# An attention and channel-mix kernel: queries kept four tokens a row, two batches turned on TensorE in FP32, finer tasks in a new order

## The chip, the cores and the metric

One core of a Trainium2 chip runs the whole program. The time is device time in microseconds (us). Executions of one kernel mostly differ by 1 to 2% (four of the kernel before took 282.42 to 286.85 us), so each run below is given as the median of its executions, beside executions of the kernel before on the same chip in the same rounds. A ratio is the mean time of one kernel's runs over that of the other's runs of the same rounds, so it is not quite the ratio of the medians quoted. Engines: PE is TensorE's matmuls, PEld its weight loads, DVE is VectorE, ACT ScalarE, POOL GpSimd. The "granted clock" is the share of TensorE's full clock that its throttle allowed.

## What the kernel computes

Eight batches of eight heads, 576 tokens, head size 64. Attention is causal in blocks of 64 tokens; its output, 512 wide, goes through a channel mix.

```python
scores = np.matmul(q, k.transpose(0, 1, 3, 2)) / np.sqrt(D)
scores = np.where(block_i >= block_j, scores, -1e9)      # blocks of 64 tokens
attn = np.exp(scores - np.max(scores, axis=-1, keepdims=True))
x = np.matmul(attn / np.sum(attn, axis=-1, keepdims=True), v)
# ... heads side by side: x is [8, 576, 512]; x_prev is x one token earlier
xk = mu_k * x + (1 - mu_k) * x_prev
xr = mu_r * x + (1 - mu_r) * x_prev
k = np.maximum(xk @ w_k, 0.0)                            # 512 -> 1024
out = sigmoid(xr @ w_r) * ((k * k) @ w_v)                # 1024 -> 512
```

## The kernel before

Every engine is given its instructions in an order that a planner writes at build time. The planner keeps a list of tasks (a few matmuls, one exponential, one load), lets them go in a simulation with guessed durations, and writes them out in that order. Five parts matter here.

**Turning.** The score matmuls take queries and keys with the head dimension on the partitions (64 partitions x 512 in the trace). Batches 2 to 7 are cast to bf16 and turned by DMA. Batches 0 and 1 (`LONGS = 2`) are cast, turned on TensorE in bf16 and copied out of PSUM:

```python
for j in range(JT):                       # add_long_qkt, batches 0 and 1
    nc.tensor.matmul(pst[:, j * D:(j + 1) * D],
                     tiles["nb", b, g, n][y * D:(y + 1) * D, j],
                     identb[...], is_transpose=True, ...)
```

**Denominators and values.** For each batch and each half (four heads), `sums()` adds up the exponentials and `part(i)` multiplies them with the values. Both use weights 32 columns wide, dealt to four column groups of TensorE, so that four small matmuls run side by side (in the trace of the kernel before, those of a group of four mostly start 3 to 5 ns apart):

```python
for t in range(3):                        # sums(): three thirds of the tokens
    ...
    for g in range(G):
        nc.tensor.matmul(PS[g * R:g * R + R, q0 - a:W3],
                         THIRD[:, (3 - t) % 3:(3 - t) % 3 + R],
                         probs(b, 4 * Q + g, kc, q0, z - q0), ...,
                         tile_position=(0, g * R))
```

This makes 119 matmuls for each batch and half. They stand in two tasks, the second free to go later.

**Normalizing** is one VectorE multiplication of a PSUM tile by the spread reciprocals, written where the channel mix reads it.

**Channel mix.** Chunks of 512 tokens: tasks of four (`w_k`, `w_r`) or eight (`w_v`) matmuls of 512 columns, 0.22 us each (0.216 us from start to start at full clock).

**Fillers.** 300 matmuls with the identity are put where TensorE would idle at the start, to keep its clock up.

## Time and profile before

| | kernel before |
|---|---|
| time | 283.6 us, median of 3 (282.59 to 286.85) |
| span of the profiled run | 282.1 us |
| TensorE busy | 93% |
| TensorE instructions in the trace (weight loads, matmuls and 12 of its sequencer) | 6,932 |
| first channel-mix matmul | 48.40 us |

The prediction below shows the lines of this profile on which it rests. The list of what TensorE waited for (what was waited for, total us, times, longest us) begins so:

```profile
PE t_s L538 <- ACT t_e L560: 3.6, 5, 1.0
PE t_m L469 <- POOL t_nl L286: 3.1, 1, 3.1
```

Each entry names what was late: another engine or a DMA. For matmuls, which this list counts, no entry of this kernel says "issue" (its weight loads, which start 0.08 us before their matmuls in the median, do have such entries, 20.7 us of them at L538). "Issue" is how the profile marks idle time for which it finds nothing that was waited for. The second part is one line of the list of DMA queues (transfers, MB, share):

```profile
q8 instruction: 27, 0.44, 0.7%
```

By its name this queue brings the program itself. It moved 27 transfers of 0.44 / 27 MB, about 16 KB each, and 6,932 TensorE instructions are 27 times 256.

### The profile page before, as it was taken

How to read it: one execution, taken by the hardware profiler on the slowest of the kernel's cores; microseconds unless marked ns; L12 is line 12 of the kernel's file. 1: busy time of each engine (PE TensorE's matmuls, PEld its weight loads, DVE VectorE, ACT ScalarE, POOL GpSimd, SP SyncE). 2: the span in 40 equal slices, each digit the busy share in tenths (PEclk: the TensorE clock that was granted, in tenths of full speed). 3: DMA queues.
4: the chain of work that ended last, by engine and by line, in shares of the span. 5: the costliest groups of instructions: out<-in, count | busy, mean ns of one | idle time of the engine just before them, and what ended most of it. 6: DMA issues, size and time to landing. Idle time of an engine off the chain costs nothing. (4 is left out here: it accounts for less than half of the span.)

```text
span 282.1 us, 8552 instructions
## 1 busy us (share of the span) xinstructions
PE 261.7 (93%) x3460; PEld 137.7 (49%) x3460; DVE 215.1 (76%) x395; ACT 186.3 (66%) x268; POOL 125.1 (44%) x262
## 2 busy tenths in 40 slices
PE   8999856898999987999999999989999999997995
PEld 8977543343445442545444545435545445543443
DVE  1663689599946986889999948893999599996432
ACT  1379778469299756875998689558865980450530
POOL 4125685076054404383475426755833532640220
PEclk9999997599999997999999999999999999999999
DMA  6999999794999899998999899999979103102113
GB/s 187 372 240 250 288 325 216 161 214 73 214 238 221 202 210 240 187 196 208 230 194 198 189 267 202 195 235 232 187 144 274 46 1 111 44 0 76 74 39 112
DMA packets 137112, 51.43 MB, mean 182 GB/s; under 512 B 127728, under 2 KB 127984, under 8 KB 137072
## 3 DMA queue, kind: packets, MB, share of 16 engines
q1 hardware_dynamic: 137072, 50.88, 77.6%
q8 instruction: 27, 0.44, 0.7%
q14 instruction: 13, 0.11, 0.1%
HBM read 33.56 MB, written 9.44 MB: 152 GB/s over the span
## 5 line engine op out<-in xcount | busy, mean ns | idle before, releaser
L560 ACT ACTIVATE t_e<-t_s 128x1024 f16<-128x1024 f32 x96 | 96.0, 1024 | 23.2 <-PE t_s L538 23.0
L786 PE MATMUL t_mm<-t_xk,WK 128*128 128x512 f16 x288 | 68.7, 383 | 1.4 <-POOL t_xk L765 0.9
L848 PE MATMUL t_mm<-WV,t_k 128*128 128x512 f16 (+1 forms) x296 | 66.8, 374 | 1.1 <-DVE t_o L858 1.0
L568 POOL MEMSET t_e<- 64x128 f16 x128 | 24.9, 210 | 73.1 <-ACT t_e L560 70.3
L796 ACT ACTIVATE t_kr<-t_mm 128x512 f32<-128x512 f32 x72 | 42.4, 599 | 17.5 <-PE t_mm L786 14.8
L848 PEld LDWEIGHTS <-t_k 128*128 128x128 f16 x296 | 27.9, 98 | 34.6 <-issue 3.8
L786 PEld LDWEIGHTS <-WK 128*128 128x128 f16 x288 | 26.2, 98 | 34.7 <-issue 7.4
L805 DVE TENSOR_TENSOR t_k<-t_kr 128x512 f16<-128x512 f32 x37 | 29.0, 796 | 18.4 <-ACT t_kr L796 18.2
L829 ACT ACTIVATE t_t<-t_mm 128x512 f32<-128x512 f32 x36 | 21.6, 600 | 31.8 <-PE t_mm L819 31.6
L819 PE MATMUL t_mm<-WR,t_xr 128*128 128x512 f16 x144 | 38.9, 401 | 1.9 <-DVE t_o L858 1.2
L538 PE MATMUL t_s<-t_qkt 64*128 64x64 bf16 (+4 forms) x384 | 34.0, 283 | 5.3 <-ACT t_e L560 3.6
L805 POOL TENSOR_TENSOR t_k<-t_kr 128x512 f16<-128x512 f32 x24 | 28.3, 1187 | 23.3 <-ACT t_kr L796 22.8
L750 DVE SCALAR_TENSOR_TENSOR t_xk<-t_d,MUK,t_xt 128x512 f16<-128x512 f32 x36 | 33.5, 945 | 3.0 <-POOL t_d L738 2.6
L858 DVE SCALAR_TENSOR_TENSOR t_o<-t_t,t_mm 128x512 f32<-128x512 f32 (+1 forms) x37 | 24.7, 666 | 12.0 <-PE t_mm L848 7.1
L750 DVE SCALAR_TENSOR_TENSOR t_xr<-t_d,MUR,t_xt 128x512 f16<-128x512 f32 x36 | 30.9, 874 | 0.0
L738 POOL TENSOR_TENSOR t_d<-t_xt 128x512 f32<-128x512 f32 x16 | 21.0, 1313 | 13.7 <-DVE t_xt L688 13.3
L538 PEld LDWEIGHTS <-t_qkt 64*128 64x128 bf16 x384 | 12.9, 95 | 27.8 <-issue 20.7
L688 DVE TENSOR_TENSOR t_xt<-t_m,t_rd 128x384 f32<-128x384 f32 (+3 forms) x42 | 22.2, 549 | 5.3 <-PE t_m L608 5.2
L608 PEld LDWEIGHTS <-VO 128*32 128x32 f16 x1264 | 23.3, 98 | 5.8 <-issue 5.3
L608 PE MATMUL t_m<-t_e,VO 128*32 128x192 f16 (+3 forms) x976 | 24.6, 243 | 0.0
L888 PE MATMUL t_mm<-identb 128*128 128x128 bf16 x300 | 21.9, 230 | 2.2 <-POOL identb masks.py:199 1.4
L819 PEld LDWEIGHTS <-t_xr 128*128 128x128 f16 x144 | 13.3, 101 | 20.7 <-issue 6.6
(58 smaller groups left out, 251.4 us busy)
## 6 DMA issues: line engine op xcount, KB each, us to landing
out_dram<-t_o SPq DMA_DIRECT2D x35, 256.0 KB, 2.9
t_vl<-in_v_dram SPq DMA_DIRECT2D x32, 256.0 KB, 4.9
t_ld<-in_q_dram SPq DMA_DIRECT2D x48, 128.0 KB, 3.6
t_ld<-in_k_dram SPq DMA_DIRECT2D x48, 128.0 KB, 3.6
t_ld<-in_q_dram SPq DMA_DIRECT2D x8, 288.0 KB, 6.7
t_ld<-in_k_dram SPq DMA_DIRECT2D x8, 288.0 KB, 6.0
t_ld<-in_moe_w_k_dram SPq DMA_DIRECT2D x8, 256.0 KB, 5.3
t_ld<-in_moe_w_v_dram SPq DMA_DIRECT2D x8, 256.0 KB, 5.0
```

The lines of the kernel that those rows point to most:

```text
L538: nc.tensor.matmul(PS[:, h, col:col + n], qkt[rows, pr, 1, kc * P:kc * P + P], qkt[rows, pr, 0, q0:q0 + n], start=True, stop=True)
L560: nc.scalar.activation(tiles["e", b, pr][:, :, i, :], tiles["ps", b, it], AF.Exp, scale=ISQ)
L568: nc.gpsimd.memset(tiles["e", b, pr][D:P, :, i, z:z + D], 0.0)
L608: nc.tensor.matmul(ps[g * R:g * R + R, q0 - a:z - a], lhs(kc, g), probs(b, 4 * Q + g, kc, q0, z - q0), start=(kc == 0 and last is not None ...
L688: nc.vector.tensor_tensor(xt_tile(c)[:, 2 * Q:2 * Q + 2, 1 + at:1 + at + w], tiles["num", b, Q, i][:, 0:2 * w].rearrange("p (s t) -> p s t ...
L750: nc.vector.scalar_tensor_tensor(tiles[name, c][:, cc], tiles["d", c, cc], (MUK1, MUR1)[n][:, cc:cc + 1], tiles["xt", c][:, cc, 1:CH + 1], ...
L786: nc.tensor.matmul(ps, WK[:, cc, jc * P:(jc + 1) * P], tiles["xk", c][:, cc], start=(cc == 0), stop=(cc == CCn - 1))
L796: nc.scalar.activation(tiles["kr", c, jc], tiles["pk", c, jc], AF.Relu)
L805: (nc.vector if eng == "DVE" else nc.gpsimd).tensor_tensor(K2, KR, KR, ALU.mult)
L819: nc.tensor.matmul(ps, tiles["xr", c][:, cc, jt * P:(jt + 1) * P], WR[:, cc], start=(cc == 0), stop=(cc == CCn - 1))
L848: nc.tensor.matmul(ps[:, 0:w], tiles["k2", c][:, jc, jt * P:(jt + 1) * P], WV[:, jc, cols], start=(jc == 0), stop=(jc == JCn - 1))
L858: nc.vector.scalar_tensor_tensor(tiles["o", c, jt, part][:, 0:w], tiles["t", c, jt][:, cols], 1.0, tiles["pv", c, jt, part][:, 0:w], ALU.a ...
```

## The change

The intent: queries are loaded with four neighbouring tokens a row (1 KB pieces) and keep that order up to the normalization, which puts the tokens back in place. Batches 0 and 1 are turned on TensorE straight from the f32 tiles, without casts. Tasks become finer, and TensorE's order is a fixed list in place of ranks. The core of the diff, with cuts marked:

```diff
-LONGS = 2
+TURNED = 2
+TENSOR = """
+q000 q001 q010 q100 q011 s000 q0t q031 s001 s0t0 q030 q021 s010 s030 q020 q1t
...                                   # 339 tasks in TensorE's order
@@ loads of queries (and of keys in batches 0 and 1)
+            return [(d[:, :].rearrange("p (h c) -> p h c", h=2),
+                     src[b, 2 * pr:2 * pr + 2, 0:CUT].rearrange(
+                         "h (p j) d -> p h (j d)", j=J))]
@@ turning batches 0 and 1
+                            nc.tensor.matmul(
+                                PS[h * D:h * D + D, j * P:j * P + P],
+                                tiles["ld", b, pr, n][:, c:c + D], identf,
+                                start=True, stop=True)
@@ denominators: four token groups in place of three thirds
-            for t in range(3):
-                            THIRD[:, (3 - t) % 3:(3 - t) % 3 + R],
+            for j in range(J):
+                for kc in range(J):
+                            FOURTH[:, (J - j) % J:(J - j) % J + R],
@@ values: three tasks of their own, and one for the denominators
-        for v, mine in enumerate(([0], [1, 2])):
+        for den, mine in (True, []), (False, [0]), (False, [1]), (False, [2]):
@@ normalizing puts the tokens back in order
+                            x[:, :, 0:w].rearrange("q s (p j) -> q s j p", j=J),
+                            num[:, :, 0:w].rearrange("q s (j p) -> q s j p", j=J),
```

Each batch and half now has 190 small matmuls on average instead of 119.

## The prediction

> **What bounds the kernel now.** I read the page first: which engine is fullest, and when.
>
> ```profile
> span 282.1 us, 8552 instructions
> PE 261.7 (93%) x3460; PEld 137.7 (49%) x3460; DVE 215.1 (76%) x395; ACT 186.3 (66%) x268; POOL 125.1 (44%) x262
> ...
> PEclk9999997599999997999999999999999999999999
> DMA  6999999794999899998999899999979103102113
> ```
>
> TensorE is the fullest engine, no other passes 76%, and the chain that ended last is TensorE almost alone. But busy is not useful work: 300 of the 3460 matmuls multiply the bf16 identity, fillers that keep the clock up. So I went to the ten-microsecond windows: after "window:" come its length, then PE, PEld, DVE, ACT and POOL busy, granted clock, DMA share, GB/s.
>
> ```profile
> 10.00:20.00 10.00, 9.60 (x189) 8.28 (x187) 5.74 (x9) 5.97 (x10) 2.20 (x4) 1.00 0.97 276
> 30.00:40.00 10.00, 5.71 (x170) 3.87 (x166) 7.86 (x19) 7.67 (x9) 8.17 (x14) 1.00 1.08 309
> 40.00:50.00 10.00, 6.23 (x166) 4.01 (x166) 9.96 (x21) 7.59 (x12) 6.21 (x13) 0.80 0.97 246
> 50.00:60.00 10.00, 9.83 (x104) 4.42 (x105) 6.34 (x14) 5.47 (x9) 2.73 (x5) 0.69 0.90 174
> 150.00:160.00 10.00, 10.00 (x162) 4.90 (x161) 9.92 (x20) 7.79 (x12) 4.41 (x12) 1.00 0.95 189
> ```
>
> From 60 us on TensorE is full: summing its windows, idle from 60 to 279 us is some 7 us. The loss is before: idle from 30 to 50 us is 8 us, and the clock falls to 0.80 and 0.69, which costs 2.0 + 3.1 = 5.1 us (1.7 us more around 105 to 115 us: 0.87 and 0.96). The timeline of TensorE says where the start goes (start, duration, line, output<-inputs, shape, count, idle before it):
>
> ```profile
> 18.75 0.61 PE L538 MATMUL t_s<-t_qkt 64*128 64x512 bf16 x6
> ...
> 35.63 0.85 PE L623 MATMUL t_mm<-t_e,THIRD 128*32 128x192 f16 x36 [0.85 <-DVE t_xt L688]
> ...
> 40.45 0.60 PE L469 MATMUL t_m<-identb,t_nl 64*128 64x64 bf16 x18 [3.07 <-POOL t_nl L286]
> ...
> 50.17 4.45 PE L819 MATMUL t_mm<-WR,t_xr 128*128 128x512 f16 x10 [0.74 <-DVE t_xr L750]
> ```
>
> The first scores come at 18.75 us, because loads of both batches stand in a row before the first keys; TensorE waits 3.07 us for a cast at 40.45; the first channel-mix matmul stands at 48.40 us. By then two batches are turned, 78 of 384 score matmuls and batch 0's values are done. Everything else fills the remaining 233.7 us almost without gaps. So the question is: **when does the channel mix start, and how much TensorE work is left from there?**
>
> Unit prices come from the full part of the same timeline:
>
> ```profile
> 168.60 0.85 PE L623 MATMUL t_m<-t_e,THIRD 128*32 128x192 f16 x36
> 169.28 0.20 PE L623 MATMUL t_m<-EL,THIRD 128*32 128x64 f16 x4
> 169.30 0.40 PE L608 MATMUL t_m<-t_e,VO 128*32 128x192 f16 x16
> 169.63 1.90 PE L786 MATMUL t_mm<-t_xk,WK 128*128 128x512 f16 x8
> 171.47 0.61 PE L538 MATMUL t_s<-t_qkt 64*128 64x512 bf16 x6
> 172.01 1.04 PE L786 MATMUL t_mm<-t_xk,WK 128*128 128x512 f16 x4
> 172.88 1.03 PE L819 MATMUL t_mm<-WR,t_xr 128*128 128x512 f16 x4
> 173.84 0.39 PE L538 MATMUL t_s<-t_qkt 64*128 64x320 bf16 x4
> ```
>
> Durations overlap, so I subtract starts. 172.01 to 172.88: four 512-column matmuls in 0.87 us, 0.216 each. 172.88 to 173.84: the same four take 0.96 when a row-tiled score follows: **a change of tiling costs about 0.095 us**. 171.47 to 172.01: two score pieces and one change, 0.22 a piece. Inside the values, four column-tiled matmuls start 3 to 4 ns apart and then the next group follows after about its columns at 2.4 per ns (192 columns: 83 ns, 64: 29 ns), so an extra small group costs 3 to 4 ns, not a full instruction.
>
> [...] the low windows follow the 30 to 50 us stretch with its 3.07 us hole. [...] packets of 256 B take about 19 ns each, those of 1 KB 47 ns and of 2 KB about 90 ns.
>
> **The change, part by part.**
>
> *Loads.* Four tokens a row make 1 KB pieces. For a 256 KB tile on 16 engines that is 256 x 47 / 16 = 0.75 us against 1024 x 19 / 16 = 1.2 us. Queries of batches 2 to 7: 24 x 0.45 = 11 us less transfer, but beside TensorE's full part: worth nothing directly. In batches 0 and 1 the old pieces were 2304 B already: no gain.
>
> *Turning batches 0 and 1.* It removes 16 casts of 0.67 to 0.75 us on the other engines and 144 bf16 transposes (29 ns apart, 4.2 us), and adds 16 tasks of 8 FP32 matmuls of 128 columns plus two tail tasks of 16 of 64 columns. [...] with one change of tiling now and then about 1 us, so 18 us in all, 14 more than before. It lands where TensorE ran 300 fillers (17 us); only 38 fillers are left in the new program.
>
> *Order of the start.* Queries and keys are loaded first, in the order of their use. The first load landed at about 4.2 us before, the next at 6 to 9.5 us. Five turns, cold at first, end near 10.5 us, so the first exponential is near 11 instead of 19.2 us. From there ScalarE goes: nine exponentials (0.93 apart), five evictions (0.6), three casts, a tail, to about 25 us; then the denominators and values of half 0 and three more exponentials of half 1, to about 30.5. Then the chain of before, with its durations: denominator 0.8, reciprocals 1.4, spreading 1.1, normalizing 1.5, difference 0.8, two mixes 1.7, small waits: the first channel-mix matmul near **39 us**. TensorE's own work up to it (18 turns, 25 scores, batch 0's values, 29 changes: 18 + 5 + 4.3 + 2.8 = 30) fits between 4 and 39, and so does the DMA (two batches of queries and keys, tails, one v, WK: some 29 us).
>
> *Left after it* (counted in the built program's order): channel mix 712 x 0.216 + 16 x 0.109 = 155.5; scores 87 of 112 tasks, 17.2 (the finer pieces add about 0.4 in all); values of seven batches, 14 x 2.18 = 30.5 (3040 matmuls instead of 1904, 284 more groups of four at 3.5 ns and some 32-column ones: +1.2 in all); 120 changes of tiling x 0.095 = 11.4 (before 127). Sum 214.6, and 3.1 us for the last product's way out (TensorE ended at 279.0 of 282.1). The same sum for the kernel before gives 213.4 + 3.1 + 6 clock + 8 idle = 230.5 against 233.7 in the trace, so it closes with 3 us unexplained.
>
> *Other engines.* Differences and squares move from VectorE to GpSimd (10 and 22 against 20 and 37 on VectorE): about 20 us off VectorE's 215, some 25 us on GpSimd's 125. With VectorE at 9.9 of 10 in many windows that takes waits away from TensorE, so I expect 4.5 us idle instead of 8.
>
> Sum: 39 + 214.6 + 3.1 + 4.5 idle + 0.5 clock + 1.5 (half the unexplained) = 263.2 us span, and 1.3 us from span to time as before (283.6 against 282.1): **264.5 us**.
>
> **The rivals.**
>
> *The FP32 halves do not run side by side, or weights are not hidden.* Then [...] TensorE bounds the start: channel mix near 50 us, about 275 us. For it: no FP32 matmul in the trace. Against: bf16 column tiles overlap there.
>
> *The start is bound by the chain through ScalarE, VectorE and the weights' DMA whatever the order.* DMA share is 0.97 to 1.08 from 10 to 50 us. Then the first channel-mix matmul stays near 46, and only clock and idle are won: about 271.
>
> *New waits in the full part.* A fixed TensorE order, one ring of four PSUM banks for values and channel mix, differences on the slower GpSimd (1.3 against 0.83 us): 10 to 15 us idle instead of 4.5, about 272.
>
> [...]
>
> **Range and chances.** The start may move by 4 us either way, idle and clock together by 5: 257 to 273. Two rivals together would be needed for less than 2% (277.9). Faster by over 2%: 0.96; within 2%: 0.03; slower: 0.01.
>
> **What would show it.** First scores near 10.5 us and first exponential near 11; first channel-mix matmul at 36 to 42 us; turning tasks about 0.9 us apart when warm, 1.7 when cold; clock 1.00 in the windows from 40 to 60 us; from there to the end about 225 us; VectorE's busy time under 200 us, GpSimd's near 150. I am wrong if the turns take 1.7 us warm, if the channel mix starts after 44 us, or if TensorE idles over 10 us behind its start.

## The result

The kernel after took **309.58 us** (median of 4, 307.1 to 311.13) against 283.1 us for the kernel before in the same rounds: ratio 1.0924, 95% interval 1.0831 to 1.1018. The prediction, 264.5 us, was wrong in size and in sign. From the page of the profile after:

```profile
span 309.0 us, 11060 instructions
PE 269.1 (87%) x4702; PEld 146.4 (47%) x4702; DVE 212.8 (69%) x426; ACT 187.6 (61%) x277; POOL 133.8 (43%) x279
...
PEclk9997786999997999789997998879999999997999
...
q8 instruction: 37, 0.61, 0.8%
```

TensorE went from 93% busy to 87%, and its clock, which in the kernel before dropped only twice before the last us (granted 0.5 from 46.0 to 56.2 and from 107.4 to 110.8 us), now drops again and again. Such stretches at 0.5 are called half clock below; in them the starts of 512-column matmuls stand 0.427 us apart, at full clock 0.216. The queue that brings the program moved 37 transfers instead of 27; TensorE's instructions grew from 6,932 to 9,417, which is 36.8 times 256. What TensorE waited for:

```profile
PE t_mm L689 <- issue: 21.8, 8, 3.8
PE t_mm L434 <- DMA t_ld<-in_q_dram: 3.8, 1, 3.8
PE t_s L604 <- ACT t_e L628: 2.7, 3, 1.1
```

The first line is new and large: eight times, 21.8 us in all, TensorE stood still inside a value task, and the profile finds no engine, buffer or transfer of data that it waited for. Two windows show it (length, then busy time of PE, PEld, DVE, ACT and POOL, granted clock, DMA share, GB/s):

```profile
90.00:100.00 10.00, 6.91 (x281) 4.07 (x267) 5.14 (x15) 2.60 (x4) 4.62 (x9) 0.83 1.11 213
200.00:210.00 10.00, 6.25 (x194) 3.79 (x180) 5.62 (x16) 2.75 (x4) 1.78 (x5) 0.83 0.32 102
```

In both, no engine is busy for 7 of the 10 us, and the clock is at 0.83. That is not the picture of an engine that waits for a slower one. TensorE's timeline shows where such a wait falls (start, duration, line, output<-inputs, shape, count, idle before it and what ended it):

```profile
91.47 0.53 PE L689 MATMUL t_mm<-t_e,VO 128*32 128x128 f16 x32
91.82 0.20 PE L689 MATMUL t_mm<-EL,VO 128*32 128x64 f16 x4
91.85 0.39 PE L689 MATMUL t_mm<-t_e,VO 128*32 128x128 f16 x14
95.33 0.32 PE L689 MATMUL t_mm<-t_e,VO 128*32 128x128 f16 x16 [3.09 <-issue]
```

A row of like matmuls breaks off in the middle and goes on 3.09 us later, with the same tiles. I then counted TensorE's instructions in the trace from 0, weight loads, matmuls and the few of its sequencer in one row (an FP32 matmul stands there as two of each). The eight waits stand before instructions number 1473, 3265, 4289, 4801, 5569, 6337, 6849 and 8897. **Each of these numbers is 256n + 449**, and in each of the eight cases the 256 instructions that end there had taken 1.1 to 2.0 us. Where there was no wait, the corresponding 256 took 2.6 us or more; in the kernel before the shortest took 5.2 us. From the start of these 256 to the end of the wait it was 3.6 to 5.2 us, and the instruction queue moved 16 KB in that time: in each of the eight cases one transfer of that queue, by its packets in the trace, began 0.7 to 2.4 us after the start of the fast block, and landed 1.3 to 1.7 us before TensorE went on.

So the first reading, an inference from these counts, was: TensorE's instructions arrive in blocks of 256, and where one was used up fast the next could be executed only some 4 to 5 us after its start (an estimate from the 3.6 to 5.2 us above). Small matmuls packed four side by side used 256 instructions in 1.1 to 2.0 us, and then there was nothing to execute. One part of this is not shown: what sets the moment of the transfer. In runs that follow, blocks used up in 1.4 us (shift, best3) and 1.65 us (half) passed without a wait; there the transfer had begun before the block did.

### The profile page after: what moved, and what is told of

The parts are those of the page before. It is cut to its first block, busy times and chain, and to the rows that moved or that the text cites.

```text
span 309.0 us, 11060 instructions
## 1 busy us (share of the span) xinstructions
PE 269.1 (87%) x4702; PEld 146.4 (47%) x4702; DVE 212.8 (69%) x426; ACT 187.6 (61%) x277; POOL 133.8 (43%) x279
## 4 chain that ended last, share of the span: by engine, by line
PE 75%; DVE 10%; issue 8%; ACT 4%; DMA 1%; POOL 1%; DVEq 0%; ACTq 0%; POOLq 0%
PE t_mm L957 20%; PE t_mm L894 19%; PE t_mm L928 9%; PE t_mm L689 9%; PE t_s L604 7%; PE t_mm L434 4%; PE t_mm L697 3%; DVE t_xk L858 2%; PE t_s L611 2%; ACT t_e L628 2%; DVE t_xt L790 2%; DVE t_xr L858 2%; DVE t_o L968 1%; ACT t_qkt L355 1%; PE t_mm L994 1%
## 5 line engine op out<-in xcount | busy, mean ns | idle before, releaser
L957 PE MATMUL t_mm<-WV,t_k 128*128 128x512 f16 (+1 forms) x296 | 73.5, 403 | 2.8 <-ACT t_k L912 2.5
L914 POOL TENSOR_TENSOR t_k<-t_kr 128x512 f16<-128x512 f32 x33 | 36.9, 1131 | 25.5 <-ACT t_kr L905 25.1
L689 PE MATMUL t_mm<-t_e,VO 128*32 128x64 f16 (+3 forms) x1568 | 32.1, 232 | 14.8 <-issue 14.3
L790 DVE TENSOR_TENSOR t_xt<-t_mm,t_rd 128x512 f32<-128x512 f32 (+3 forms) x44 | 34.3, 833 | 10.8 <-PE t_mm L689 9.6
L846 POOL TENSOR_TENSOR t_d<-t_xt 128x512 f32<-128x512 f32 x26 | 28.9, 1124 | 19.8 <-DVE t_xt L790 15.0
L604 PE MATMUL t_s<-t_qkt 64*128 64x128 bf16 (+3 forms) x256 | 33.4, 322 | 2.7 <-ACT t_e L628 2.7
L914 DVE TENSOR_TENSOR t_k<-t_kr 128x512 f16<-128x512 f32 x22 | 18.0, 831 | 22.1 <-ACT t_kr L905 22.0
L858 DVE SCALAR_TENSOR_TENSOR t_xk<-t_d,MUK,t_xt 128x512 f16<-128x512 f32 x36 | 30.3, 865 | 4.1 <-POOL t_d L846 4.1
L765 DVE RECIPROCAL t_c<-t_mm 128x128 f32<-128x128 f32 x16 | 15.2, 953 | 21.2 <-PE t_mm L689 21.2
L611 PE MATMUL t_s<-t_qkt 64*128 64x64 bf16 x320 | 23.5, 199 | 1.0 <-ACT t_e L628 1.0
L604 PEld LDWEIGHTS <-t_qkt 64*128 64x128 bf16 x256 | 12.8, 98 | 18.9 <-issue 15.2
```

The costliest lines, as they stand in the source:

```text
L604: nc.tensor.matmul(PS[:, h, col:col + J * w].rearrange("p (j n) -> p j n", j=J), keys, ask[:, 0:CUT].rearrange("d (j p) -> d j p", j=J)[:, ...
L611: nc.tensor.matmul(PS[:, h, col:col + D], keys, ask[:, CUT:S], start=True, stop=True)
L689: nc.tensor.matmul(ps, lhs, e, start=start, stop=stop, tile_position=(0, g * R))
L790: nc.vector.tensor_tensor(x[:, :, 0:w].rearrange("q s (p j) -> q s j p", j=J), num[:, :, 0:w].rearrange("q s (j p) -> q s j p", j=J), rd[: ...
L846: (nc.vector if eng == "DVE" else nc.gpsimd).tensor_tensor(tiles["d", c, cc], x[:, cc, 1:CH + 1], x[:, cc, 0:CH], ALU.subtract)
L858: nc.vector.scalar_tensor_tensor(tiles[name, c][:, cc], tiles["d", c, cc], (MUK1, MUR1)[n][:, cc:cc + 1], tiles["xt", c][:, cc, 1:CH + 1], ...
```

## The experiments

**Theory A**: TensorE runs out of instructions where small matmuls stand close together, and the stalls lower its clock. **Rival B**: the start, with few fillers, is cold and late, and the rest follows. **Rival C**: slower work on VectorE, with strided operands, makes TensorE wait. **Rival D**: the number of instructions as such costs time, whatever their spacing.

### shift: the same program, block boundaries moved

```diff
+    def tiny():
+        ps = new("mm", [P, CH], FP)
+        for x in range(64):
+            nc.tensor.matmul(ps[0:32, 0:32], identb[:, 0:32], identb[:, 0:32], ...)
+    plan.add("PE", 2.0, tiny, takes=[wbuf], name="w")    # first on TensorE
```

> The kernel after, with 64 tiny matmuls (32 x 32, 128 instructions counting their weight loads) put first on TensorE, so that every later TensorE instruction's number grows by 128. Theory A (TensorE runs out of instructions, which arrive in blocks of 256): the idle stretches ended by 'issue' stay just before instructions numbered 256n+449, and so move to other tasks: near 32, 67, 103, 191, 202, 221 and 231 us in place of 39, 92, 124, 134, 161, 188, 201 and 257; 6 to 9 of them, 15 to 24 us in sum; time 309 +-6. Rival C (the waits belong to the value tasks and the engines that feed them): the same tasks stall at the same times as in the kernel after, within 2 us, and the numbers before which they stall are no longer 256n+449.

Measured: 314.19 us (ratio 1.1103, 1.1038 to 1.1168). The trace's list of waits:

```profile
PE t_mm L689 <- issue: 20.0, 8, 3.7
...
PE t_s L604 <- issue: 2.8, 1, 2.8
```

All waits of over 1.5 us marked "issue" again stand before instructions numbered 256n + 449, now in other places: 35, 69, 103, 137, 169, 207 and 238 us. I had named 3 of these 7 places to within 3 us; which blocks are fast enough to stall depends on where the boundary cuts the tasks. One of the waits now falls on a score task (L604), which had none before. A wait that moves when 64 useless matmuls are put in front, keeps to the number and not to the task, and also hits another kind of task belongs to the supply of instructions. Rival C in its plain form falls.

### split: more instructions, but spaced as before

```diff
@@ kernel before, sums() and products()
-                    nc.tensor.matmul(ps[...q0 - a:z - a], lhs, probs(q0, z - q0), ...)
+                    for lo, hi in ((q0, mid), (mid, z)):      # two halves
+                        nc.tensor.matmul(ps[...lo - a:hi - a], lhs, probs(lo, hi - lo), ...)
```

> The kernel before, with each matmul of the denominators and values cut into two of half the columns: about 9,900 TensorE instructions in place of 6,932, more than the 9,404 of the kernel after, but in the order of the kernel before. Theory A (256 instructions used up in under about 2.1 us): only where the start packs them, 1 to 4 'issue' stalls of 2 to 4 us, and a time of 288 to 297. Rival D (the number of instructions as such, whatever their spacing): at least the 8 stalls of the kernel after, and 300 or more. If instructions cost nothing beyond their columns: 283 to 287 and no stall.

Measured: executions of 292.96, 292.94, 295.28 and 288.12 us. Three of the four count as slow, being over 1.5% above the fastest, so no ratio is given; the profile is of one of these, and I read from it where TensorE stalls, not the time. 9,940 TensorE instructions, more than in the kernel after, and:

```profile
PE t_mm L623 <- issue: 3.9, 1, 3.9
...
PE t_mm L608 <- issue: 2.6, 2, 2.1
```

Three stalls, all between 33 and 46 us, where the start packs these tasks, all before a number 256n + 449. From there to the end, where some 8,200 of the 9,940 instructions stand, there is none. Spacing decided here, not number: rival D falls.

### half: fewer small matmuls for the same columns

```diff
-            for j in range(J):                 # 4 groups, up to 128 columns each
+            for j in range(2):                 # 2 pairs, up to 256 columns each
...
-                            probs(b, 4 * Q + g, kc, kc * 32, M)[:, j],
+                            probs(b, 4 * Q + g, kc, kc * 32, M)[:, 2 * j:2 * j + 2],
...
-                    nc.vector.reciprocal(tiles["c", b, Q], PS[:, 0:M])
+                    nc.vector.reciprocal(tiles["c", b, Q], PS[:, 0:2 * M])
```

> The kernel after, with the denominators summed for two token groups a matmul in place of one: 32 matmuls of up to 256 columns in place of 64 of up to 128 for each batch and half, so 1,024 instructions fewer for the same columns; the reciprocal before the spreading has 256 columns in place of 128, about 0.9 us more in each of 16 places (VectorE + 15 us). Theory A: stalls fall from 8 to 4 to 6, the denominators no longer standing beside them, and the time falls to 296 to 305 although VectorE works more. Rival C (VectorE's chain of reciprocal and normalizing carries the loss): VectorE's 15 us come on top, 312 to 325.

Measured: 301.71 us (1.0660, 1.0613 to 1.0707), 8 us below the kernel after, although VectorE's busy time rose from 212.8 to 219.9 us:

```profile
PE t_mm L690 <- issue: 8.4, 5, 3.0
```

Less VectorE work is not what the kernel lacked.

### norm_in: the stride of the normalization's write

```diff
-  x[:, :, 0:w].rearrange("q s (p j) -> q s j p", j=J)      # write every 4th
+  x[:, :, 0:w].rearrange("q s (p j) -> q s p j", j=J)      # write in a row
```

> The kernel after, with the normalizing multiplication going through its elements in the order of the output (contiguous write, strided reads) in place of the order of the input (contiguous reads, write every fourth element); same result. Theory A: stalls as in the kernel after (7 to 9, 18 to 25 us), time 303 to 310 even if the 128x512 form falls from 1091 ns to about 700 (VectorE 14 us less). Rival C: if it falls to about 700 ns, the time falls by 8 us or more, to 301 or less, with the stalls no longer where they were. If it stays near 1091 ns, the write's stride isn't the cost and the run says nothing on C.

Measured: 308.55 us (1.0905, 1.0851 to 1.0959); the 128x512 form fell only from 1091 to 1048 ns. In the kernel before it took 679. So by its own terms this run says little on C; it only shows that the direction of the stride is not what makes the operation slower.

### respace: only the order of TensorE's tasks changed

If A holds, putting other tasks between the small matmuls must bring most of the loss back, with the work of every engine unchanged. I searched offline for an order in which no block of 256 instructions is used up too fast. The program is the kernel after, apart from the list. (From this list the planner derives the order on the other engines too, and it put 92 fillers into the start in place of 38. So the edit is the list alone, but what follows from it is a little more.)

```diff
 TENSOR = """
-q000 q001 q010 q100 q011 s000 q0t q031 ...
+q000 q001 q110 q030 q100 q0t s000 q010 ...       # 310 tasks moved by up to 26 places
```

> The kernel after with only the order of its TensorE tasks changed (310 tasks moved by up to 26 places), so that other tasks stand between the small matmuls of the denominators and values: counted from the built program with the prices of the trace, no block of 256 instructions from number 256n+192 is shorter than 2.3 us (after: eight under 2.0). It has 65 more changes of tiling, 65 x 0.095 = 6 us. Theory A: at most 2 'issue' stalls, under 3 us in sum, the half-clock stretches that followed them gone too; 309.6 - 20 (stalls) - 10 (clock) + 6 = 286, range 282 to 292. If the loss lies elsewhere (rival B the start, rival C the strided and slower work of VectorE): 300 or more, since the work of every engine is the same.

Measured: **293.15 us** (1.0362, 1.0308 to 1.0417), 16 us below the kernel after.

```profile
PE 266.7 (92%) x4756; PEld 142.9 (49%) x4756; DVE 215.0 (74%) x426; ACT 189.7 (65%) x277; POOL 138.4 (48%) x279
...
PEclk9999999999999997999999999999999999999999
```

The waits marked "issue" shrank to 2.4 us, the granted clock rose from 0.939 to 0.994, and VectorE, ScalarE and GpSimd executed as many instructions as before, in 2 to 5 us more of busy time. Of the 19.3 us between the two spans, 18.4 lie behind the first channel-mix matmul, where no filler stands. That is the main cause, taken away; burst4, below, puts it into the kernel before. Rival B falls as the main cause: the first channel-mix matmul, at 49.96 us, is nearly as late as in the kernel after (50.83). But I had expected 286 and at most 292; some 7 us of the gain did not come, and the kernel is still slower than the one before.

### half_respace: both

The diffs of half, and an order spaced in the same way.

> The denominators with half as many matmuls, and an order spaced in the same way (no block of 256 under 2.8 us; 65 more changes of tiling than the kernel after). Theory A: no 'issue' stall; 301.7 - 8.4 (its stalls) - 5 (clock) + 6 = 294, range 287 to 299; it stays above the respaced kernel if VectorE's 12 us more now count, and at or under it if they don't.

Measured: 294.85 us (1.0429, 1.0376 to 1.0481), with three short stalls of 2.5 us in sum where none was expected. It is no better than respace. Whether fewer instructions gain nothing more once the spacing is right, or VectorE's longer reciprocals took the gain back, the run cannot tell.

### burst, fewwide and burst4: the stall by itself

To see the stall and its effect on the clock apart from this change, I put 256 tiny matmuls at the head of one channel-mix task in each of five chunks of the kernel before. As a control, 18 wide matmuls stood in the same places.

```diff
             ps = tiles["pk", c, jc] = new("mm", [P, CH], FP)
+            if jc == 3 and 2 <= c <= 6:
+                for x in range(256):                             # burst
+                    nc.tensor.matmul(ps[0:32, 0:32], identb[:, 0:32], identb[:, 0:32], ...)
+                # fewwide instead: 18 matmuls of 512 columns
+                # burst4 instead: g = 32 * (x % 4); ps[g:g + 32, 0:32], tile_position=(0, g)
```

> The kernel before, order untouched, with 256 tiny matmuls (32 x 32; 512 instructions) put at the head of one channel-mix task in each of five chunks, about 3.8 us of TensorE work each if they run at 15 ns. Theory A: in every burst at least one 'issue' stall of 2 to 4 us, before an instruction numbered 256n+449, and half-clock stretches after them; 315 to 332 in all, 15 us or more above the run with few wide matmuls in the same places. If closely spaced instructions cost only their own time: within 4 us of that run and no stall.

> The control of the burst: in the same five places 18 matmuls of 512 columns (36 instructions, 3.9 us). Both theories: 5 x 3.9 = 19.5 us over the kernel before, less what other engines' waits give back, 296 to 304; no 'issue' stall.

Measured: burst 317.49 us (1.1226, 1.1164 to 1.1288), fewwide 303.33 us (1.0715, 1.0658 to 1.0772). The 14 us between them are what was hoped for, but not for the expected reason: the burst did not stall. Its matmuls stood 26 ns apart, not 15 as I had guessed, so each burst was 6.7 us of plain work instead of 3.9, and 5 x 2.8 is the 14 us. At 26 ns a matmul, 256 instructions take 3.3 us, and that was slow enough (0.4 us of "issue" in all five bursts together). So I packed them as the values are packed:

> The burst again, in the kernel before and in the same five places, but with the 256 tiny matmuls dealt to four column groups, as the denominators and values of the kernel after are, so that they run side by side: in the burst before they stood 26 ns apart, 256 instructions in 3.3 us, and nothing stalled; in column groups 256 instructions should take 1 to 2 us. Theory A: in each burst one 'issue' stall of 2 to 4 us before an instruction numbered 256n+449, 300 to 315 in all. If supply weren't the limit: 282.7 + 5 x (1.8 to 3.6) = 292 to 301 and no 'issue' stall.

Measured: 316.0 us (1.1136, 1.1033 to 1.1240). The groups of the two runs, burst first (count, busy us, mean ns, idle before and its end):

```profile
L787 PE MATMUL t_mm<-identb 128*32 128x32 bf16 x1280 | 33.4, 176 | 0.5 <-issue 0.4
```

```profile
L788 PE MATMUL t_mm<-identb 128*32 128x32 bf16 x1280 | 12.6, 183 | 15.7 <-issue 15.7
```

The same 1280 matmuls, dealt to four column groups, take 12.6 us instead of 33.4, and TensorE then waits 15.7 us for instructions: the two programs come out within 2 us of each other. There are six stalls, one or two to a burst, each before an instruction numbered 256n + 449, of 1.7 to 3.2 us. One of them on the timeline, inside a burst:

```profile
111.76 2.10 PE L788 MATMUL t_mm<-identb 128*32 128x32 bf16 x215
117.02 0.47 PE L788 MATMUL t_mm<-identb 128*32 128x32 bf16 x41 [3.16 <-issue]
```

The clock is the second finding of this pair. In burst, the trace has no half-clock stretch in or behind any of the five bursts. In burst4, half-clock stretches of 3.4 to 6.8 us begin at 118.2, 152.3, 186.4 and 254.7 us, each inside a stall or within 1.5 us of its end; only the stall at 219 us has none. So at four of these five bursts a stall cost twice: its own length, and up to half of the stretch at half clock. The total came out at 316 where I had said 300 to 315.

### noturn_re: does turning on TensorE bring anything?

```diff
-TURNED = 2
+TURNED = 0        # and the 18 q tasks taken out of respace's list
```

> The respaced kernel with batches 0 and 1 turned by DMA as batches 2 to 7 are, their 18 FP32 tasks taken out of TensorE's order (the rest of it unchanged; no block of 256 under 2.2 us). If turning on TensorE brings the start forward as the prediction had it (first scores at 10 in place of some 19 us), the first channel-mix matmul moves from 51.9 to 56 or later and the time from 293 to 297 or more. If the start hangs on the chain through ScalarE, VectorE and the loads whatever turns the keys: within 3 us, 290 to 296.

Measured: 315.53 us (1.1083, 1.0989 to 1.1177); first channel-mix matmul at 61.58 us, and

```profile
PE t_s L603 <- DMA t_qkt<-NB: 24.1, 3, 14.4
```

With this order, the DMA turns come too late. The run shows that the turning matters to an order made for it; it does not compare the two ways at their best.

### evict_in: are ScalarE's slow copies what holds the start?

```diff
@@ respace, copy of turned keys out of PSUM
-  return (dst.rearrange("q (p j) -> q j p", j=J), PS[:, :].rearrange("q (j p) -> q j p", j=J))
+  return (dst.rearrange("q (p j) -> q p j", j=J), PS[:, :].rearrange("q (j p) -> q p j", j=J))
```

> The respaced kernel with the copies of turned keys out of PSUM going through their elements in the order of the output (write contiguous, reads strided). On ScalarE that copy took 1.15 us and more for keys against about 0.6 for queries in the kernel after; eight of them stand in the start. If the stride of the write is the cost, ScalarE's copies of keys fall to about 0.6 us, the denominators of the second half (38.2 us) come 1 to 3 us sooner, and the time falls by 1 to 4 us, to 289 to 292. If the start isn't bound by ScalarE there: 293 +-1 whatever the copy takes.

Measured: 292.89 us (1.0267, 1.0154 to 1.0380). ScalarE's copies on average, first in respace's parent (the kernel after; in respace itself the mean is 1166 ns), then here:

```profile
L355 ACT CAST t_qkt<-t_mm 128x512 bf16<-128x512 f32 x8 | 8.9, 1147 | 7.6 <-PE t_mm L434 7.6
```

```profile
L355 ACT CAST t_qkt<-t_mm 128x512 bf16<-128x512 f32 x8 | 4.5, 581 | 5.9 <-PE t_mm L434 5.9
```

The copy halved, so here the stride of the write is the cost, but the denominators of the second half stood at 38.0 us (38.2 in respace) and the time did not move clear of noise. ScalarE's copies alone are not what holds the start.

### best3, best4 and morefill: order of the small tasks; the clock of the start before

best3 and best4 carry both contiguous writes, and another order and another choice of engine for casts, squares and differences, from a longer offline search. morefill is the kernel before with more fillers:

```diff
-FILL = 150
+FILL = 220
```

> The kernel after with another order of TensorE's tasks (311 moved by up to 22 places, 45 more changes of tiling), another choice of engine for the casts, squares and differences, and both strided writes made contiguous. If the start hangs on the order in which VectorE, GpSimd and ScalarE are given their small tasks: first channel-mix matmul 1 to 3 us sooner than the respaced kernel (50 us), few stalls, 281 to 287. If it hangs on something else: 50 to 52 again and 289 to 294.

> As best3, with another order and choice of engines (319 tasks moved by up to 30 places): first channel-mix matmul near 48 us, 281 to 287, if the order of the small tasks is what holds the start; 50 to 52 and 289 to 294 if not.

> The kernel before with 440 filler matmuls in place of 300, the added ones falling in the idle places between 30 and 48 us; nothing else changed. If the clock costs what the half-clock stretch at 46 us suggests (10.2 us at half: 5.1 us), it falls to 278 +-1.5, with the windows from 40 to 60 us at 0.95 or more. If the fillers themselves hold up useful work (each waits its turn on TensorE), 282 to 286.

Measured: best3 **283.90 us** (1.0029, 1.0005 to 1.0052), best4 286.22 us (1.0108, 1.0082 to 1.0134), morefill 284.02 us (1.0013, 0.9989 to 1.0037). The first channel-mix matmul came at 52.66, 49.42 and 51.25 us. best3 makes up for the loss to within 0.3% of the kernel before, but not by an earlier start. Its first exponential is at 17.5 us, not 11, and its channel mix starts later than in the kernel after; what it has is a full part almost without idle time (3.0 us in gaps of over 0.4 us after 52 us, where the kernel after has 23.8). It changes order, engines and both writes at once; which of them brought the 9 us beyond respace is not shown. morefill did give TensorE a full clock:

```profile
40.00:50.00 10.00, 8.38 (x188) 7.23 (x188) 8.16 (x20) 7.12 (x11) 3.93 (x8) 1.00 0.81 234
50.00:60.00 10.00, 10.00 (x174) 5.42 (x171) 7.79 (x16) 8.29 (x14) 4.51 (x10) 1.00 0.90 177
```

(0.80 and 0.69 before), and won nothing. The fillers may have taken back on TensorE what the clock gave; the run cannot tell that from a clock that is hidden by other waits. Either way, the 5.1 us that the prediction took for a loss to be had cannot be had so.

### lightw, lightw_b3, norecip and norecip_b: loads, or VectorE's chain?

All four are wrong in their results on purpose. lightw and lightw_b3 (on respace and best3) load a quarter of each weight tile and repeat it. norecip and norecip_b (on respace and the kernel before) leave out the reciprocals and their spreading for batch 0.

```diff
@@ lightw, lightw_b3
-  (d[:, 0:C], src[half, cc] ...)
+  (d[:, 0:P], (src[half, cc] ...)[:, 0:P])          # the cast repeats it 4 times
@@ norecip, norecip_b
+                    if b == 0:
+                        return                      # in recip() and spread()
-                    rd = tiles["rd", b, Q]
+                    rd = tiles["rd", b, Q] if b else RD1      # ones
```

> The respaced kernel with each weight load fetching only its first 128 of 512 columns, and the casts repeating them (the result is wrong on purpose; every instruction and its order stays, 3.9 MB of the 5.2 MB of weights aren't moved in the first 50 us). If the loads hold the start: first channel-mix matmul from 50 to 46 us or less, time from 293 to 285 to 290. If the chain through VectorE, GpSimd and ScalarE holds it: 49 to 51 us and 291 to 294.

> The same with the order and engines of best3 (283.9, first channel-mix matmul at 52.7 us). If the loads hold the start: 48 us or less and 277 to 281. If not: 52 to 53 us and 282 to 285.

> The respaced kernel without the reciprocals and their spreading for batch 0, which is multiplied by ones instead (result of batch 0 wrong on purpose; all other instructions and their order stay). It takes 2 x 2.1 us of VectorE's work out of the start. If VectorE's work for the two halves, one after the other, holds the first channel-mix matmul: from 50 to 45 to 47 us, and the time from 293 to 287 to 290. If not: 49 to 51 us and 292 to 294.

> The same taken out of the kernel before (2 x 2.05 us). If VectorE holds its start too: first channel-mix matmul from 48.4 to 44 to 46.5 us, time from 283.3 to 278 to 281. If not: within 1 us of the kernel before.

Measured:

| run | time us | ratio, 95% | first channel-mix matmul |
|---|---|---|---|
| lightw | 290.78 | 1.0283 (1.0233 to 1.0333) | 51.11 us (respace 49.96) |
| lightw_b3 | 283.71 | 1.0022 (0.9994 to 1.0050) | 50.93 us (best3 52.66) |
| norecip | 292.31 | 1.0306 (1.0251 to 1.0360) | 49.48 us (respace 49.96) |
| norecip_b | 283.32 | 0.9999 (0.9965 to 1.0032) | 50.24 us (before 48.40) |

None moves the start by more than 2 us, or the time by more than 2.4. The traces show why one cut at a time does not. In lightw, VectorE is almost without a gap from 36 to 51 us. In norecip it has gaps, and they are casts that stand in front of the normalization in VectorE's fixed order and wait for their own loads:

```profile
42.61 0.43 DVE L363 CAST WK<-t_ld 128x512 f16<-128x512 f32 x1 [0.95 <-DMA t_ld<-in_moe_w_k_dram]
44.33 0.43 DVE L363 CAST NB<-t_ld 128x512 bf16<-128x512 f32 x1 [1.29 <-DMA t_ld<-in_q_dram]
44.67 1.08 DVE L796 TENSOR_TENSOR t_xt<-t_mm,RD 128x512 f32<-128x512 f32 x1
```

The normalization at 44.67 had its operands, but came behind them. Take away the loads, and VectorE's work fills the time; take away that work, and the loads fill it. This speaks for at least two chains of about the same length through the start, tied together by the engines' fixed orders; no run cut two at once. Which of them would have to be cut together to win the 10 us stays open.

## Why the prediction was wrong

**Turning in FP32.** Right in size, though the 1 us a task was my estimate, for which the kernel before, without an FP32 matmul, showed nothing. Measured, from the start of a task of eight FP32 matmuls to the next start on TensorE: 0.87 to 1.03 us warm. The first two, which began before 7.0 us, took 1.73 and 1.62 us where the next followed directly: their pairs of column halves start 0.213 us apart up to there and 0.109 us after (in the kernel before, the fillers too start 0.107 us apart until 5.0 us and 0.056 us after). The two halves of a pair start 6 to 18 ns apart when warm, so they do run side by side. First scores 9.89 us (predicted 10.5), first exponential 11.05 (11). Right.

**"First channel-mix matmul near 39 us."** Wrong by 12 us: 50.83. Two terms failed. The denominators of the second half were to follow at 30.5 us and stand at 38.04; they sit behind these two lines of TensorE's timeline:

```profile
26.61 0.28 PE L697 MATMUL t_mm<-t_e,FOURTH 128*32 128x128 f16 x8
29.05 1.16 PE L697 MATMUL t_mm<-t_e,FOURTH 128*32 128x64 f16 x56 [2.16 <-POOL t_e L637]
...
38.04 0.79 PE L697 MATMUL t_mm<-t_e,FOURTH 128*32 128x128 f16 x64
...
50.83 1.31 PE L894 MATMUL t_mm<-t_xk,WK 128*128 128x512 f16 x4
```

Three scores of the second half stand behind the first half's denominators in the new order, which wait 2.16 us for GpSimd; and nine exponentials and ScalarE's other work took until 29.0 us, not 25. Then the "chain of before, with its durations", 8.5 us, took 12.8 (38.04 to 50.83). The kernel before says the same: from 35.63 to 48.40 us it is 12.8 there too. I summed the durations on the chain and left out the other half's mixes and the casts that share VectorE with it. The distance itself stood in the lines that I had quoted.

**"An extra small group costs 3 to 4 ns."** This is the step that turned a gain into a loss. As TensorE time nothing in the runs speaks against it: best3, whose stalls are small, needs 283.5 - 52.66 = 230.8 us from its first channel-mix matmul to the end; the prediction's span of 263.2 less 39, 224.2, plus 45 more changes of tiling at 0.095 makes 228.5. But I priced small matmuls in columns and never in instructions. 3,040 of them at this spacing outrun the supply: 21.8 us of stalls, none foreseen.

**"Idle 4.5 us" and "clock 0.5 us."** Behind its start the kernel after has 19.0 us of stalls (21.8 less the 2.8 of the one at 42 us) and seven half-clock stretches of 3.4 us, 23.9 us at half speed, which is 11.9 lost. (Six of them come with a stall, of 2.0 to 3.75 us, and begin inside it or within 1.5 us of its end; the seventh, at 280.1 us, comes with a wait of 2.5 us for ScalarE. Behind the shortest stall, 1.84 us, none came; behind the stall at 42 us one began 2.5 us later, after another wait.) 224.2 + 19.0 + 11.9 = 255.1, against 309.0 - 50.83 = 258.2 in the trace. So behind the start, supply and clock account for nearly all of the miss, and respace shows it from the other side: it needs 289.8 - 49.96 = 239.8 us there. In the start itself, one stall and 13.6 us at half clock cost little here: half, norm_in, respace and evict_in, with and without such a stall, all start the mix between 50 and 52 us. That is no rule: shift, with a stall of 3.7 us at 35 us, starts it only at 53.8 us. It is part of why respace fell short of 286: with the stall and the lost clock gone, the start was only 0.9 us earlier.

**Other engines.** VectorE was to fall below 200 us and is at 212.8: casts and differences did leave it, but the 128x512 normalization takes 1091 ns instead of 679. GpSimd is at 133.8, not 150. (A slip in the sum: 283.6 - 282.1, from span to time, is 1.5 us, not 1.3.)

**The rivals.** "FP32 halves not side by side" and "start bound by the chain" were named; the second was half right (it gave 46 us, and nothing for the start was won). "New waits in the full part" had the right place and about half of the size (10 to 15 us idle against 23.8), for another reason. None of them was the supply of instructions.

What would have shown it beforehand: the queue line with its 27 transfers for 6,932 instructions (37 for 9,417 in the kernel after), and a count of how fast the new program uses up 256 instructions (1 to 2 us in eight places, 5 us and more before).

## What to carry to other kernels

Price a TensorE program in instructions as well as in columns: where small matmuls run side by side, count how long each run of 256 instructions lasts, and lengthen the short ones by putting wide matmuls between the small. (In these runs the eight that took 1.1 to 2.0 us in the kernel after all ended in a wait; the kernel before, at 5.2 us and more, has no such wait; in other runs blocks of 3 to 5 us sometimes had one, up to 2.1 us. Some 5 us is thus an estimate of what is safe.) Idle time marked "issue", in the middle of like instructions, is the mark of it; the proof is to shift the program by half a block and see the stalls keep to the instruction number. And before a gain at the start is counted, find all chains that run through it: here cutting one at a time, in six ways, won at most 2.4 us.
